# Windowed attention with a gated feed-forward: where the first unit's queries are issued, and on which engine a weight's first decoding step may run

## The chip, the cores and the metric

The kernel runs on one core of one Trainium2 chip. The metric is device time in microseconds (us). The median of three runs of the kernel before is 1043.59 us (1042.27 to 1043.75).

## The reference

```python
scores = scale * q @ k.T                       # 8 batches, 8 heads, 576 tokens, 64 wide
mask = (rel >= 0) & (rel < 128)                # rel = query position - key position
scores = where(mask, scores - slopes[h] * abs(rel), -1e9)
attn = exp(scores - max(scores)); attn = attn / (sum(attn) + 1e-9)
x = (attn @ v), heads side by side             # 4608 tokens x 512
out = (sigmoid(x @ w_gate) * (x @ w_val)) @ w_out   # 512 -> 1536 -> 512
```

The queries, keys and values are float32. The three weights are float64 and reach the chip as pairs of 32-bit words.

## The kernel before

The program works on 32 attention units; a unit is one batch and one pair of heads, laid out as nine blocks of 128 columns (1152 columns). For each unit it loads keys (`kr`, 576 KB), queries (`qr`, 320 KB) and values (`vr`, 288 KB). PE computes the scores of four blocks at a time in the early units (L387), DVE merges the two halves of the window (L400) and reduces (L408), ACT takes the exponential (L411), ACT or DVE scales (L431, L432), PE transposes three blocks (L436), ACT or DVE copies them out (L181, L182), POOL spreads them over a triangle layout (L447), and PE multiplies with the values (L473). The unit's result goes to DRAM (`xs`).

The feed-forward runs in three passes over the hidden units. The first takes 2 of 12 slices of the weights while the attention is still running (L523 for gate and value, L561 for the output projection): its matmuls fill PE's gaps. The two others take 5 slices each and all tokens, with a Strassen-like product (L667) and the output projection (L561).

A slice of a weight is a float64 tile of 128x512 that has to be decoded into float32 first. `decode` (L291) loads the raw words into one of two buffers (`wraw`), scales the high words on ACT (L300), shifts them left on DVE (L301), and or-s bits from the low and the high words in on DVE (L304, twice). Then the value is split into two parts: a cast (L181 on ACT or L182 on DVE) and a subtraction (L190). The tile `wbits`, of which there are two, is free again after the subtraction. 36 slices are decoded: 6 for the first pass, 15 for each later one.

The order of all instructions is written by a planner, `Graph` (L61 to L150), before the program is built. Each operation has a due time (`want`), a cost, and one or more ways, that is engines with a cost each. `order` (L97) is greedy: among all operations whose inputs are planned, it takes the one with the smallest key. The key holds the start time on the engine, the cost above the cheapest way, and a small penalty (0.1 for DVE) for a way that is not the first:

```python
key = (s + cost - least + (YIELD[e] if k else 0.0), o.want, o.seq)
...
gap = (o.start - free["PE"] - 0.2) // (0.25 if free["PE"] > 5.0 else 0.45)
...
moved = max(moved, o.start + 1.7) + o.size
```

Where PE would sit idle early in the plan, the planner puts filler matmuls of the identity there (`warm`, L246), so many as fit its own gap. A DMA's landing is planned from one running total of bytes (`moved`, L127) at 220 KB per us of plan (350 for weights). All DMAs are issued by `move` (L185) on SP's queue, in the order of the plan. The planner knows nothing of the set-up that DVE does at the start (L215 to L232), nor of ACT's table load.

`load` (L354) issues a unit's loads. For the first unit, keys and queries come in two parts each, cut at block 3; the values follow. The scores of blocks 0 to 3 read the keys of blocks 0 to 3, so they need both parts of the keys and the first part of the queries; blocks 4 to 7 need the second part of the queries too.

Of the kernel before, what the change touches and what calls it, by code (L numbers as in the profile page):

```python
# [19 lines left out]
NBLK = TOK // P  # L20
DM, DFF = 512, 1536
# [30 lines left out]
def as32(ap):  # L52
    return ap.bitcast(F32)
# [97 lines left out]
def dve_cost(n, psum=False, two=False):  # L151
    return 0.07 + n * (0.00104 if psum or two else 0.00053)


def act_cost(n, psum=False):
    return (0.05 if psum else 0.1) + n * 0.00084
# [3 lines left out]
def attention_gated_ffn(ctx: ExitStack, tc: tile.TileContext, qd, kd, vd, wg, wv, wo, out):  # L160
    nc = tc.nc
    ctx.enter_context(tc.manual_schedule())
    g = Graph()
# [10 lines left out]
    def T(pool, name, shape, dtype, tag=None):  # L174
        if name not in made:
            made[name] = pool.tile(shape, dtype, tag=tag or name, name=name)
        return made[name]
# [4 lines left out]
              ways=[("DVE", dve_cost(n, psum), not psum, lambda: nc.vector.tensor_copy(out(), src()))])  # L182


    def move(out, src, reads, writes, want, kb, fast=False, release=0.0):  # L185
        g.add("SP", 0.6, lambda: nc.sync.dma_start(out(), src()), reads, writes, want, size=kb / (350.0 if fast else 220.0), release=release)

    def minus(out, a, b, n, reads, writes, want, psum=False, pool=True):
        way = ("POOL", 0.1 + n * 0.00223, True, lambda: nc.gpsimd.tensor_tensor(out(), a(), b(), op=ALU.subtract))
# [101 lines left out]
    def decode(src, fc, bits, kb, keys, want, release=0.0):  # L291
        s = raws[0] % NRAW
        raws[0] += 1
        kr = ("wraw", s)
        if src.dtype == F32:
            move(lambda: as32(bits()), lambda: src[fc], keys, [kb], want, 256, False, release)
            return
        raw = lambda: T(moe, f"wraw{s}", [P, DM, 2], I32)
        move(lambda: raw().rearrange("p f t -> p (f t)"), lambda: src[fc].bitcast(I32), [], [kr], want, 512, True, release)
        g.add("ACT", act_cost(DM), lambda: nc.scalar.mul(as32(bits()), as32(raw()[:, :, 1]), 2.0 ** -112), [kr, *keys], [kb], want)  # L300
        g.add("DVE", dve_cost(DM), lambda: nc.vector.tensor_scalar(  # L301
            bits(), bits(), 3, None, op0=ALU.logical_shift_left), [], [kb], want, port=True)
        for word, scalar, o0 in ((0, 29, ALU.logical_shift_right), (1, -0x80000000, ALU.bitwise_and)):
            g.add("DVE", dve_cost(DM, two=True), lambda word=word, scalar=scalar, o0=o0: nc.vector.scalar_tensor_tensor(  # L304
                bits(), raw()[:, :, word], scalar, bits(), op0=o0, op1=ALU.bitwise_or), [kr], [kb], want, port=True)
# [7 lines left out]
    def prepare(w, src, kind, i, want):  # L313
        sb = bitn[0] % 2
        bitn[0] += 1
        bits = lambda: T(moe, f"wbits{sb}", [P, DM], I32)
        kb = ("wbits", sb)
        decode(src, w.fcs[i], bits, kb, w.keys(FC2), want)
        parts(lambda: w.tile(kind, 0)[:, i], lambda: w.tile(kind, 1)[:, i], lambda: as32(bits()), DM, [kb, *w.keys(FC2)],
              (w.name, kind, 0, i), (w.name, kind, 1, i), want)  # L320
# [32 lines left out]

    def load(u):  # L354
        want = u.when(-NBLK)
        cuts = (0, 3, NBLK) if u.n == 0 else (0, NBLK)
        for h, (b0, b1) in enumerate(zip(cuts, cuts[1:])):
            sl, q0, q1 = slice(b0 * P, b1 * P), (b0 + 1) // 2, (b1 + 1) // 2
            move(lambda sl=sl: kraw(u)[:, sl], lambda sl=sl: kd[u.b, u.p, :, sl], [], [("kr", u.l, i) for i in range(b0, b1)],
                 want, 64 * (b1 - b0))  # L360
            move(lambda q0=q0, q1=q1: qraw(u)[:, q0:q1], lambda q0=q0, q1=q1: qd[u.b, u.p, :, q0:q1], [],
                 [("qr", u.l, i) for i in range(2 * q0, 2 * q1)], want, 64 * (q1 - q0))
        move(lambda: vraw(u), lambda: vd[u.b, u.p], [], [("vr", u.l)], want, 288)


# [233 lines left out]
    def prepare2(w, i, want, release=0.0):  # L599
        s = bitn[0] % 2  # L600
        bitn[0] += 1
        kg, kt = ("wbits", s), "tt"
        gt = lambda: T(moe, f"wbits{s}", [P, DM], I32)
        tt = lambda: T(moe, "tt", [P, 6, 2 * P], F32)
        decode(wg, w.fcs[i], gt, kg, w.keys(i), want, release)
        decode(wv, w.fcs[i], lambda: tt()[:, 0:2].rearrange("p a f -> p (a f)").bitcast(I32), kt, w.keys(i), want, release)
        g0, g1, v0, v1 = (lambda: as32(gt())[:, 0:2 * P], lambda: as32(gt())[:, 2 * P:], lambda: tt()[:, 0], lambda: tt()[:, 1])
        t = [lambda k=k: tt()[:, 2 + k] for k in range(4)]
        for o, a, b in ((t[0], v0, g0), (t[1], v1, t[0]), (t[2], v1, v0), (t[3], g1, t[1])):
            minus(o, a, b, 2 * P, [kg], [kt], want)  # L610
        for a, b, src, k in ((0, 2, lambda: as32(gt()).rearrange("p (a f) -> p a f", a=2), kg), (2, 7, lambda: tt()[:, 1:], kt)):
            parts(lambda a=a, b=b: w.tile2(i, 0)[:, a:b], lambda a=a, b=b: w.tile2(i, 1)[:, a:b], src, (b - a) * 2 * P,
                  [k, *w.keys(i)], ("w2", i, 0, a), ("w2", i, 1, a), want)
# [105 lines left out]
    for n in range(NSLOT - 1):  # L719
        load(units[n])  # L720
    at = 0
    for u in units:
        if u.n + NSLOT - 1 < len(units):
            load(units[u.n + NSLOT - 1])
        while at < (u.n + 1) * NBLK:
            n = RUN // 2 if at < SOON * NBLK else RUN
            scores(stream[at:at + n])
            at += n
        if u.n == 0:
            todo = [(src, kind, i) for i0 in range(0, FC1, GRP) for src, kind in ((wg, "g"), (wv, "v")) for i in range(i0, i0 + GRP)]  # L730
            for k, (src, kind, i) in enumerate(todo + [(wo, "o", i) for i in range(FC1)]):
                prepare(w1, src, kind, i, W0 + WSTEP * k)
        if u.p == NPAIR - 1:
            while todo1 and (todo1[0] + 1) * NB <= (u.b + 1) * S:
                if todo1[0] >= LATE and banks[0] == 2:
                    banks[0] = 8
                    g.add("PY", 0.0, lambda: None, [], [TP, TAIL], FIRST)
                ffn(todo1.pop(0), w1)
# [84 lines left out]
```

## Time and profile before

| | us |
|---|---|
| median of three runs | 1043.59 |
| the profiled execution | 1042.42 |
| its span, first to last instruction | 1040.7 |
| PE busy | 1026.2 |
| DVE busy | 732.0 |
| ACT busy | 530.6 |
| POOL busy | 115.8 |

The span is what lies between the first and the last instruction of the profiled execution; the execution's own time holds 1.7 us more. Busy time is the union of an engine's instructions. A busy PE is not a PE at its peak, since the ends of matmuls are modelled; filler matmuls count as busy too. The granted clock of TensorE was 1.0 of full speed (the 2.4 GHz level) in every stretch. A matmul of float32 in the attention leaves two records in the trace. In the rows below, "x16" after an operation is the number of records, and the bracket at the end of a row of the timeline is the idle time of the engine just before it and what ended it.

### The profile page before, as it was taken

To read this page: it belongs to the slowest core of one execution; us is meant where nothing else is said; L and a number is where in the kernel's file an instruction comes from. 1 tells how busy PE (TensorE), PEld (TensorE's weight loads), DVE (VectorE), ACT (ScalarE), POOL (GpSimd) and SP (SyncE) were. 2 spreads that over 40 slices of the span, in tenths; PEclk is the share of its full clock that TensorE was granted. 3 is DMA by queue.
4 is the path that set the end of the run, shared out by engine and by line. 5 is a ranking of instruction groups with operands and counts; after the bars stand their busy time and mean duration, and the time that the engine had idled before them with its cause. 6 is when DMAs were issued, how large, how long until landed. Compare 5 with 4: busy or idle time off the path is not lost.

```text
span 1040.7 us, 17441 instructions
## 1 busy us (share of the span) xinstructions
PE 1026.2 (99%) x6024; PEld 913.4 (88%) x6024; DVE 732.0 (70%) x2031; ACT 530.6 (51%) x1477; POOL 115.8 (11%) x208
## 2 busy tenths in 40 slices
PE   9899999999999999999999999999999999999998
PEld 7677788787878998989899999989898989999897
DVE  7998888798899884554746475999556474747352
ACT  6898688898945551524334243635243333415140
POOL 2333233443411000000000000010000000000000
PEclk9999999999999999999999999999999999999999
DMA  8757577856556615041412305261503122040303
GB/s 285 250 191 262 184 249 223 297 168 254 184 192 213 222 51 182 1 152 31 137 47 81 102 17 186 82 233 52 163 20 118 65 96 88 26 157 1 122 1 102
DMA packets 74729, 142.70 MB, mean 137 GB/s; under 512 B 7312, under 2 KB 30224, under 8 KB 74640
## 3 DMA queue, kind: packets, MB, share of 16 engines
q1 hardware_dynamic: 74640, 141.58, 40.8%
q8 instruction: 47, 0.77, 0.3%
q14 instruction: 42, 0.34, 0.1%
HBM read 103.81 MB, written 37.75 MB: 136 GB/s over the span
## 4 chain that ended last, share of the span: by engine, by line
PE 88%; DVE 7%; ACT 3%; issue 1%; DMA 0%; POOL 0%; SPq 0%; ACTq 0%; DVEq 0%; POOLq 0%
PE mm L667 38%; PE mm L561 26%; PE mm L523 9%; PE mm L473 5%; PE mm L387 5%; PE mm L436 3%; ACT pb L411 1%; DVE wbits L304 1%; DVE mm L674 1%; ACT both L181 0%; DVE w2s L190 0%; DMA kr<-in_k_dram 0%; DVE hidden L190 0%; DVE tt L190 0%; DVE tt L304 0%
## 5 line engine op out<-in xcount | busy, mean ns | idle before, releaser
L667 PE MATMUL mm<-later,w2s 128*128 128x384 f32 x1800 | 332.0, 334 | 0.0
L667 PEld LDWEIGHTS mm<-later,w2s 128*128 128x128 f32 x1800 | 314.7, 188 | 1.1
L561 PE MATMUL mm<-w2o,hidden 128*128 128x512 f32 x1080 | 249.2, 390 | 0.0
L561 PEld LDWEIGHTS mm<-w2o,hidden 128*128 128x128 f32 x1080 | 202.4, 188 | 40.8
L678 ACT ACTIVATE sg<-mm 128x384 f32<-128x384 f32 x120 | 59.0, 493 | 145.6 <-PE mm L667 98.6
L181 ACT COPY a<-mm 128x384 f32<-128x384 f32 x60 | 28.8, 480 | 195.2 <-PE mm L667 194.5
L447 POOL TENSOR_SCALAR_AFFINE_SELECT pt<-both 128x384 f32<-128x384 f32 x192 | 105.0, 571 | 180.3 <-ACT both L181 164.0
L523 PE MATMUL mm<-first 128*128 128x512 f32 x432 | 111.6, 401 | 0.0
L566 DVE SCALAR_TENSOR_TENSOR ob<-mm,pi 128x512 f32<-128x512 f32 x72 | 49.5, 689 | 72.8 <-PE mm L561 39.0
L523 PEld LDWEIGHTS mm<-first 128*128 128x128 f32 x432 | 77.8, 188 | 15.5 <-issue 1.0
L674 DVE TENSOR_TENSOR mm<-mm,a 128x384 f32<-128x384 f32 x60 | 33.8, 564 | 75.6 <-PE mm L667 75.6
L411 ACT ACTIVATE pb<-pb,st 128x128 f32<-128x128 f32 x216 | 84.7, 398 | 2.5 <-DVE st L408 2.3
L667 PE MATMUL mm<-xc,w2s 128*128 128x384 f32 x360 | 73.0, 337 | 0.2 <-DVE p L674 0.2
L667 PE MATMUL mm<-later_o,w2s 128*128 128x384 f32 x360 | 72.3, 335 | 0.0
L473 PEld LDWEIGHTS mm<-pt,vr 128*64 128x64 f32 x832 | 61.2, 137 | 12.7 <-issue 8.7
L473 PE MATMUL mm<-pt,vr 128*64 128x256 f32 (+2 forms) x832 | 67.4, 306 | 0.6 <-POOL pt L447 0.6
L667 PEld LDWEIGHTS mm<-xc,w2s 128*128 128x128 f32 x360 | 63.4, 188 | 1.8 <-DVE p L674 0.8
L667 PEld LDWEIGHTS mm<-later_o,w2s 128*128 128x128 f32 x360 | 63.2, 188 | 0.5 <-ACT u L181 0.5
L181 ACT COPY both<-mm 128x384 f32<-128x384 f32 x95 | 45.2, 475 | 27.4 <-PE mm L436 16.6
L561 PE MATMUL mm<-first_o,early_h 128*128 128x512 f32 x216 | 57.1, 402 | 1.2 <-ACT early_h L181 0.7
L387 PE MATMUL mm<-kr,qr 64*128 64x256 f32 (+1 forms) x396 | 55.4, 382 | 0.2 <-DMA kr<-in_k_dram 0.2
L400 DVE COPY_PREDICATED mm<-early_h,mm 128x256 f32<-128x256 int32 (+1 forms) x144 | 49.0, 391 | 8.8 <-PE mm L387 8.3
(117 smaller groups left out, 1347.9 us busy)
## 6 DMA issues: line engine op xcount, KB each, us to landing
part<-ob SPq DMA_DIRECT2D x72, 256.0 KB, 4.3
pi<-part SPq DMA_DIRECT2D x72, 256.0 KB, 3.3
later_xr<-xs SPq DMA_DIRECT2D x16, 768.0 KB, 4.7
kr<-in_k_dram SPq DMA_DIRECT2D x21, 576.0 KB, 5.0
vr<-in_v_dram SPq DMA_DIRECT2D x32, 288.0 KB, 3.3
xs<-xt SPq DMA_DIRECT2D x32, 288.0 KB, 3.0
out_dram<-ob SPq DMA_DIRECT2D x36, 256.0 KB, 2.1
qr<-in_q_dram SPq DMA_DIRECT2D x21, 320.0 KB, 5.3
```

What stands on the lines that cost most here:

```text
L181: g.add("ACT", act_cost(n, psum), lambda: nc.scalar.copy(out(), src()), reads, writes, want, release=release, ways=[("DVE", dve_cost(n, ps ...
L387: nc.tensor.matmul(sp[bank_of(r, a)][:, a % 2, lo:], qraw(u)[rows, i // 2], kraw(u)[rows, (i - 1) * P + lo:(i + 1) * P], start=True, stop= ...
L400: g.add("DVE", dve_cost((a1 - a0) * P, psum=True), lambda b=b, a0=a0, a1=a1: nc.vector.copy_predicated(sp[b][:, a0:a1, P:], before[:, a0:a ...
L411: g.add("ACT", 0.39, lambda: nc.scalar.activation(pb()[:, e], pb()[:, e], AF.Exp, bias=st()[:, e:e + 1], scale=-1.0, accum_out=st()[:, 3 + ...
L447: nc.gpsimd.affine_select(pt(u)[:, f0:f0 + 2 * n - 1:2, :], both(), [[0, n], step], cmp, 0.0, base=0, channel_multiplier=mult)
L473: nc.tensor.matmul(to()[e * D:(e + 1) * D, a - e * S - t0:b - e * S - t0], vraw(u)[:, c], seen, start=first, stop=last, skip_group_check=True)
L523: nc.tensor.matmul(mm[s], w.tile(kind, wi)[:, i, c * P:(c + 1) * P], x()[:, c, :], start=(k == 0 and c == 0), stop=(k == 2 and c == KC - 1))
L561: nc.tensor.matmul(mm[s], hcol(x, i, w is w1)[:, ts], w.tile("o", wi)[:, i, :], start=(i == 0 and k == 0), stop=(i == n - 1 and k == 2))
L566: g.add("DVE", dve_cost(DM, psum=True), lambda: nc.vector.scalar_tensor_tensor(ob(), mm[s], 0.5, pi(), op0=ALU.mult, op1=ALU.add), [("mm", ...
L667: nc.tensor.matmul(mm[b][:, 0:N2], w.tile2(i, wp)[:, wk, c * P:(c + 1) * P], combo(k, xp)[:, c], start=(start and c == 0 and j == 0), stop ...
L674: g.add("DVE", dve_cost(N2, psum=True), lambda: nc.vector.tensor_tensor(o(), bk(b)(), a(), op=ALU.add), [("mm", b), *reads] if okeys else ...
L678: g.add("ACT", act_cost(N2, psum=True), lambda: nc.scalar.activation(sg[h](), bk(b)(), AF.Tanh, scale=0.5), [("mm", b)], [("sg", h)], F)
```

## The change

The first unit's keys and queries are loaded in three parts each, cut at blocks 2 and 4. Its query loads are issued from ACT's queue, all other loads stay on SP. And the first step of decoding gets a second way: beside ACT, the planner may put it on DVE.

```diff
-    def move(out, src, reads, writes, want, kb, fast=False, release=0.0):
-        g.add("SP", 0.6, lambda: nc.sync.dma_start(out(), src()), reads, writes, want, size=kb / (350.0 if fast else 220.0), release=release)
+    def move(out, src, reads, writes, want, kb, fast=False, release=0.0, queue="SP"):
+        start = nc.sync if queue == "SP" else nc.scalar
+        g.add(queue, 0.6, lambda: start.dma_start(out(), src()), reads, writes, want, size=kb / (350.0 if fast else 220.0), release=release)
...
-        g.add("ACT", act_cost(DM), lambda: nc.scalar.mul(as32(bits()), as32(raw()[:, :, 1]), 2.0 ** -112), [kr, *keys], [kb], want)
+        scaled = lambda: (as32(bits()), as32(raw()[:, :, 1]), 2.0 ** -112)
+        g.add("ACT", act_cost(DM), lambda: nc.scalar.mul(*scaled()), [kr, *keys], [kb], want,
+              ways=[("DVE", dve_cost(DM), True, lambda: nc.vector.tensor_scalar_mul(*scaled()))])
...
-        cuts = (0, 3, NBLK) if u.n == 0 else (0, NBLK)
+        cuts = (0, 2, 4, NBLK) if u.n == 0 else (0, NBLK)
+        queue = "ACT" if u.n == 0 else "SP"
...
-                 [("qr", u.l, i) for i in range(2 * q0, 2 * q1)], want, 64 * (q1 - q0))
+                 [("qr", u.l, i) for i in range(2 * q0, 2 * q1)], want, 64 * (q1 - q0), queue=queue)
```

In the planner's costs the step takes 0.53 on ACT (`act_cost(512)`) and 0.34 on DVE (`dve_cost(512)`). The parts of the keys are now 128, 128 and 320 KB, those of the queries 64, 64 and 192 KB; before they were 192 and 384, and 128 and 192 KB.

## Rows read from the trace of the kernel before

**Rows 1.** Busy time of each engine in stretches of the whole program: the stretch and its length, then busy us and number of instructions for PE, PEld, DVE, ACT and POOL, the granted clock, the share of the DMA engines and GB/s.
```profile
0.00:20.00 20.00, 18.41 (x127) 15.04 (x129) 15.22 (x88) 10.45 (x42) 4.70 (x15) 1.00 0.84 303
20.00:60.00 40.00, 35.69 (x297) 26.68 (x293) 37.62 (x188) 37.00 (x149) 14.29 (x25) 1.00 0.73 246
60.00:150.00 90.00, 87.15 (x668) 69.20 (x668) 78.11 (x404) 75.63 (x296) 31.62 (x61) 1.00 0.65 217
150.00:250.00 100.00, 100.00 (x780) 80.53 (x779) 83.66 (x430) 85.62 (x320) 39.81 (x74) 1.00 0.75 252
...
300.00:640.00 340.00, 339.96 (x1746) 312.63 (x1745) 221.14 (x359) 132.45 (x258) 4.47 (x4) 1.00 0.35 116
640.00:710.00 70.00, 69.85 (x375) 65.92 (x374) 68.08 (x121) 38.76 (x72) 3.95 (x3) 1.00 0.45 149
```

**Rows 2.** The chain of work that ended last, in order of time, one of its longest pieces: start, length, what.
```profile
408.94 35.49 PE mm L667 x204
```

**Rows 3.** The same chain in its first 13 us.
```profile
1.71 4.73 DMA kr<-in_k_dram
...
6.48 1.66 PE mm L387 x10
8.14 2.88 PE mm L246 x24
...
11.79 1.11 PE mm L387 x7
```

**Rows 4.** SP's instructions at the start, in order of time: the issue of the first unit's loads. Start, length of the issue, what.
```profile
0.80 0.38 SPq L186 DMA_DIRECT2D kr<-in_k_dram  x1
...
1.71 0.42 SPq L186 DMA_DIRECT2D kr<-in_k_dram  x1
2.17 0.43 SPq L186 DMA_DIRECT2D qr<-in_q_dram  x1
2.65 0.43 SPq L186 DMA_DIRECT2D vr<-in_v_dram  x1
```

**Rows 5.** PE before the first scores, from the timeline; and the second part of the queries in the list of DMA issues (size, us from issue to landing).
```profile
1.43 3.78 PE L246 MATMUL mm<-ident 128*128 128x128 f32 x16 [1.43 <-POOL ident masks.py:199]
...
qr<-in_q_dram SPq DMA_DIRECT2D x1, 192.0 KB, 4.8
```

**Rows 6.** ACT and DVE at the start, from the timeline: ACT's table load, the end of DVE's set-up, DVE's first work on scores, ACT's first exponential.
```profile
0.80 1.28 ACT L411 ACT_TABLE_LOAD   x1 [0.80 <-PEq L807]
...
4.33 1.30 DVE L232 TENSOR_SCALAR early_h<-early_h 128x640 f32<-128x640 f32 x3
...
6.36 0.30 DVE L400 COPY_PREDICATED mm<-early_h,mm 128x128 f32<-128x128 int32 x1 [0.73 <-PE mm L387]
...
7.88 0.40 ACT L411 ACTIVATE early_h<-early_h,st 128x128 f32<-128x128 f32 x1 [5.80 <-DVE st L408]
```

**Rows 7.** The timeline from 13 to 19 us: ACT's two longest waits there, and PE's filler between them.
```profile
13.37 0.48 ACT L181 COPY both<-mm 128x384 f32<-128x384 f32 x1 [1.50 <-PE mm L436]
...
14.32 2.27 PE L246 MATMUL mm<-ident 128*128 128x128 f32 x18
...
18.65 0.48 ACT L181 COPY both<-mm 128x384 f32<-128x384 f32 x1 [1.05 <-PE mm L436]
```

**Rows 8.** The chain of work that ended last between 20 and 25 us: the first step of decoding on it.
```profile
21.16 0.57 ACT wbits L300
...
24.23 0.57 ACT wbits L300
```

**Rows 9.** DVE between 24 and 39 us, from its timeline: its two idle times, the last decoding step of the first weight and that weight's cast; and ACT's first steps of decoding at 39.83 and 44.05.
```profile
24.26 0.28 DVE L426 TENSOR_SCALAR st<-st 128x3 f32<-128x3 f32 x1 [0.60 <-ACT pb L411]
...
31.31 0.68 DVE L304 SCALAR_TENSOR_TENSOR wbits<-wraw,wbits 128x512 int32<-128x512 int32 x1
...
36.58 0.27 DVE L426 TENSOR_SCALAR st<-st 128x3 f32<-128x3 f32 x1 [0.47 <-ACT pb L411]
...
38.29 0.42 DVE L182 CAST first<-wbits 128x512 fp32r<-128x512 f32 x1
...
39.83 0.69 ACT L300 ACTIVATE wbits<-wraw 128x512 f32<-128x512 f32 x1
...
44.05 0.65 ACT L300 ACTIVATE wbits<-wraw 128x512 f32<-128x512 f32 x1
```

**Rows 10.** The first two decoding steps by their lines, over the whole program: count, then shortest, median and longest in ns, first and last start in us.
```profile
L300 ACT ACTIVATE wbits<-wraw x26: 648/672/706, 21.1 to 712.9; 128x512 f32<-128x512 f32 x26
...
L301 DVE TENSOR_SCALAR wbits<-wbits x26: 398/419/741, 21.8 to 713.8; 128x512 int32<-128x512 int32 x26
```

**Rows 11.** The chain of work that ended last from 643 to 704 us: its first piece on DVE, one of L301 and one of L304; and PE's row of the timeline where the chain goes back to PE.
```profile
643.58 0.57 DVE mm L674
...
659.35 0.34 DVE wbits L301
...
660.15 0.60 DVE wbits L304
...
703.79 1.31 PE L667 MATMUL mm<-xc,w2s 128*128 128x384 f32 x6 [0.15 <-DVE p L674]
```

**Rows 12.** The first step of decoding in the stretch from 640 to 720 us.
```profile
L300 ACT ACTIVATE wbits<-wraw x8: 661/680/703, 642.9 to 712.9; 128x512 f32<-128x512 f32 x8
L300 ACT ACTIVATE tt<-wraw x4: 667/676/681, 649.3 to 688.9; 128x512 f32<-128x512 f32 x4
```

## The prediction

> **What bounds the kernel now.** I read the busy time by stretch first [rows 1]. From 150 to 250 us PE is busy all the time, from 300 to 640 for 339.96 of 340 us, from 640 to 710 for 69.85 of 70. Its pace there is a full one: the chain of waits has 204 matmuls of one kind in 35.49 us [rows 2], 174 ns each with nothing between. PE's work is fixed by the reference, so a change can shorten the program only where PE has holes or plays filler. That is the beginning: PE is idle 1.59 us before 20 us, 4.31 us from 20 to 60, 2.85 us from 60 to 150. Before 20 us much of "busy" is warm-up matmuls (L246), which compute nothing. In 20 to 60 us ACT has 37.00 and DVE 37.62 of 40 us: these two, not PE, are the bound of the head, and from about 150 us on everything is shifted by whatever the head takes.
>
> Second, the chain of waits at the start [rows 3]. It goes through the landing of the second part of the keys (to 6.44 us), the ten matmuls that need it, 24 filler matmuls for 2.88 us, and then the next scores at 11.79. The first part of the keys is not on it. Third, the issue times on SP [rows 4], and what PE, DVE and ACT do until then [rows 5 to 7]. Fourth, the chain from 20 to 45 us and where the weights' first step (L300) stands in it [rows 8, 9]. Last, the stretch from 643 to 704 us, where the second set of weights is decoded [rows 11].
>
> **The change, part by part. Loads of the first unit.** Five DMAs on SP (keys, queries, keys, queries, values) become four on SP (keys of 2, 2 and 5 blocks, values) and three on ACT (queries). Costs: three issues of about 0.43 us [rows 4] on ACT. ACT loads its table until 2.08 us and then waits 5.80 us for DVE [rows 6], so 1.3 us of issuing is hidden; without that cover it would cost 1.3 us. SP's later issues come one slot, 0.47 us, sooner (the values at 2.17 and not 2.65 us).
>
> What the first four blocks need shrinks from 704 KB (all but the last queries) to 384 KB. DVE, however, is in its set-up until 5.63 us (4.33 + 1.30) and now starts on the scores at 6.36 [rows 6]. So it gains at most 0.73 us there; with less waiting behind it, the first exponential on ACT comes some 1.2 us before 7.88. This is not on the chain. The chain needs blocks 4 to 7, that is the last keys and queries, and these complete the same 896 KB as before. After them PE plays filler up to the time at which the planner expects the second unit's queries; its transfer model gets the same bytes in the same order up to there, so the expected time stays. The gain on the path is what the second landing gains. The queries landed at about 6.97 (issued at 2.17, 4.8 us to landing) [rows 4, 5]. Their issue moves from 2.17 to about 1.7 us if ACT issues ahead of its table load (0.80 plus two slots of 0.46): up to 0.5 us sooner. If the table load goes first, the third issue is at 2.08 + 2 x 0.46, about 3.0 us, 0.8 us later than now. In front of the filler a further gap or two is rounded down, worth about one filler matmul of 0.24 us (two records of 0.12, 2.88 us by 24) [rows 3]. I take -0.3 us, ends -0.5 and +0.8: nearer to the gain, because the last keys keep their issue time of 1.71 with 64 KB less in them.
>
> A rule speaks against this part. The Trainium skill, "DMA: Bandwidth & Descriptors", section "Issuing engines are not separate DMA queues", says that transfers issued by different engines share the same 16 DMA engines and that a second issuer saves only issue time. Issue time alone would be the -0.5 us end, bytes alone would be 0; no row here shows two issuers.
>
> **The first step of decoding.** A weight of 128x512 takes one step on ACT (L300, median 672 ns, 0.57 us of its chain at a time), one on DVE (L301, 419 ns) and two more (L304) [rows 8, 10]. The first step may now run on DVE. No row shows that; the nearest are L301 (one source, contiguous) and L304 (two sources, every other word): 0.34 us in DVE's full queue, as L301's piece of the chain, to 0.60, as L304's [rows 11]. I take 0.34, as the step has one source.
>
> The Trainium skill, "VectorE: DVE Perf Modes", section "What auto-detection actually checks", lets one-source instructions from and to SBUF run at two elements a cycle on conditions that name the outermost dimension and not the step. By that the strided step costs what L301 does; no row here shows a strided one-source step.
>
> The planner takes DVE when DVE is free no later than 0.09 us after ACT (0.53 - 0.34 on ACT against a penalty of 0.1). Where DVE's queue is full, ACT keeps the step. The ACT way also gets a handicap of 0.19 in the key that it did not have, so the step is passed over while ACT has ready work. Behind it wait L301, L304, the cast and the subtraction, and then the buffer. In the head this is covered: the cast of the first weight runs at 38.29, 6.3 us after its last decode step (31.31 + 0.68) [rows 9].
>
> Of six such steps in the head, two lie on the chain while ACT carries it, 0.57 us each at 21.16 and 24.23 [rows 8]. DVE was idle 0.60 us before 24.26 and 0.47 before 36.58 [rows 9], room for two steps of 0.34 (0.68 in 1.07). Two more (39.83, 44.05) run while DVE carries the chain; if moved, they cost 0.34 each. So the ends are -1.14 and +0.68. I take one of the two moved with profit: -0.6 us.
>
> After 150 us: 0. PE has no holes, and what ACT saves there, nobody waits for.
>
> **The order itself.** The planner is greedy; another way in one step reorders hundreds after it. This can give back or lose part of PE's holes from 20 to 150 us (4.31 + 2.85 = 7.2 us) [rows 1]. No row tells which sign; I count a quarter, 1.8 us, as an error on both sides.
>
> **The sum.** -0.3 - 0.6 = -0.9 us. The profiled execution took 1042.42 us (span 1040.7 and 1.7 around it): it would be 1041.5. The median of the three runs stands 1.17 us above that execution, so I put the forecast at 1043.59 - 0.9 = 1042.7 us. Alone it has 1040.6 to 1044.8 (1.8 us of order, and some of the other ends).
>
> **Rivals.** (a) *The change does nothing to the path*: the second landing stays at about 7 us, because bytes and not issue times set it, and the planner leaves the steps of the head on ACT, as DVE's queue is as full as ACT's (37.62 against 37.00 of 40 us) [rows 1]. Time 1043.6. For it: filler fixed by the planner [rows 3]. Against it: DVE does have the two gaps [rows 9].
>
> (b) *The head packs better than I count*: both early steps leave ACT (-1.14), the landing gains its 0.5, and transposes of the first blocks, done sooner, take away one of ACT's early waits (1.50 us at 13.37, 1.05 at 18.65) [rows 7], say 1.05. Together -2.7: 1040.9 us. Against it: at 14.32 PE plays filler again for the planner's expected transfers [rows 7], which keeps the early pace.
>
> (c) *Slower: DVE becomes the bound at 643 to 704 us.* There DVE has 68.08 of 70 us [rows 1], the chain runs along DVE from 643.58 until PE, at 703.79, has waited 0.15 us for DVE [rows 11]: DVE has no slack left against PE. Each step that the planner gives to DVE here costs 0.34 us of the end. It decides from about six such steps (2.1 us); with all twelve of the stretch [rows 12] it is 4.1 us: 1047.7. Against it: with a full DVE queue the key prefers ACT, which has 38.76 of 70 us.
>
> **How the numbers follow.** Forecast 0.45 (of it 0.04 below and 0.02 above the bounds), (a) 0.17, (b) 0.25 (0.01 within), (c) 0.13 (0.02 within). A measurement of this kernel can tell about 0.2%, 2.1 us, from no change: below 1041.5 is faster, above 1045.7 slower. That gives faster 0.28, same 0.59, slower 0.13. The predicted time is that of the forecast, 1042.7 us. The range reaches down over (b), with its order error partly, to 1039.6 and up to 1045.6, which leaves out most of (c) and the deepest part of (b), 2 in 10.
>
> **What would show it.** In the profile after: queries issued on ACT, at about 0.8 us or behind the table load; ten filler records in place of 16 ahead of the first scores [rows 5] (the planner's gap there falls from 3.8 to 2.3 us of its own time, five matmuls of 0.45 where there were eight); the first exponential near 6.7 us; the scores of the second unit still at 11 to 12 us. L301's line and the first step on DVE at about 0.42 us each; in the head one to three of six on DVE; from 643 to 704 few or none. PE idle from 20 to 60 us down by about a microsecond. It is wrong if the scores of the second unit come over 1 us sooner, if PE waits for DVE near 700 us, or if PE's holes up to 150 us change by over 2 us through order alone.

## The result: 6.4 us slower

| | before | after |
|---|---|---|
| median of 6 runs, us | 1042.22 (1041.8 to 1043.75) | 1048.57 (1046.8 to 1050.44) |
| profiled execution, us | 1042.42 | 1047.89 |
| its span, us | 1040.7 | 1046.2 |

The ratio is 1.0063, 95% interval 1.0053 to 1.0074: slower by over 0.2%, and outside the range of the prediction.

**Where the time is lost.** Busy time of each engine by stretch, the changed kernel, columns as in [rows 1]; one more stretch is shown, 360 to 380 us, in which PE was busy for all 20.00 us before.
```profile
0.00:20.00 20.00, 17.57 (x122) 14.42 (x122) 14.47 (x87) 10.97 (x42) 3.96 (x14) 1.00 0.81 289
20.00:60.00 40.00, 35.75 (x285) 26.81 (x283) 35.54 (x194) 36.79 (x155) 14.96 (x27) 0.96 0.72 248
60.00:150.00 90.00, 86.63 (x682) 69.14 (x679) 77.33 (x392) 72.31 (x271) 34.67 (x64) 1.00 0.66 215
150.00:250.00 100.00, 98.41 (x769) 78.26 (x768) 83.47 (x423) 83.85 (x318) 40.27 (x69) 1.00 0.72 240
250.00:300.00 50.00, 49.51 (x341) 40.22 (x340) 42.27 (x159) 35.78 (x121) 19.07 (x30) 1.00 0.49 171
...
360.00:380.00 20.00, 18.80 (x105) 17.58 (x104) 18.05 (x30) 9.98 (x21) 0.00 (x0) 1.00 0.47 151
...
640.00:710.00 70.00, 70.00 (x373) 65.87 (x372) 62.90 (x109) 36.40 (x66) 6.24 (x4) 1.00 0.45 147
```
The kernel before from 250 to 300 us, a stretch that [rows 1] don't show:
```profile
250.00:300.00 50.00, 48.18 (x340) 38.57 (x335) 43.61 (x142) 37.91 (x117) 16.92 (x28) 1.00 0.43 143
```
PE's holes grow by 0.84 us before 20 us and by 0.52 from 60 to 150; from 20 to 60 they stay, but the clock is below 1. From 150 to 250 there are 1.59 us of holes where there were none, and from 250 to 300 they shrink from 1.82 to 0.49. At 360 to 380 us there are 1.20 us of holes where there were none. From 640 to 710, the stretch of the prediction's rival (c), PE is busier than before.

Holes in a timeline can understate a wait, since the ends of matmuls are modelled. Two landmarks measure it in another way: when PE is done with the first pass, and how long the next 60 matmuls, all of the second pass, take from start to start. First the kernel before, PE's timeline at the change of passes.
```profile
349.09 1.23 PE L667 MATMUL mm<-later,w2s 128*128 128x384 f32 x6
350.15 2.92 PE L561 MATMUL mm<-first_o,early_h 128*128 128x512 f32 x12
352.91 10.59 PE L667 MATMUL mm<-later,w2s 128*128 128x384 f32 x60
363.34 1.20 PE L667 MATMUL mm<-later_o,w2s 128*128 128x384 f32 x6
```
The changed kernel, the same view (L667 is L671, L561 is L565).
```profile
349.51 5.64 PE L565 MATMUL mm<-first_o,early_h 128*128 128x512 f32 x24
354.98 8.74 PE L671 MATMUL mm<-later,w2s 128*128 128x384 f32 x48
363.97 0.62 PE L671 MATMUL mm<-later,w2s 128*128 128x384 f32 x2 [0.25 <-ACT later L181]
365.50 2.32 PE L671 MATMUL mm<-later,w2s 128*128 128x384 f32 x10 [0.92 <-DVE later L191]
367.67 1.20 PE L671 MATMUL mm<-later_o,w2s 128*128 128x384 f32 x6
```
Before, the first pass ends at 350.15 + 2.92 = 353.07 us; less the 1.06 us in which six matmuls of the second pass had been done ahead, 352.0. After, it ends at 349.51 + 5.64 = 355.15: **3.1 us late**. Then the next 60 matmuls take 363.34 - 352.91 = 10.43 us before and 367.67 - 354.98 = 12.69 after: **2.3 us more**. Together that is the whole loss of this execution: the chain's last run of output projections starts at 1016.54 before and 1021.90 after, 5.4 us later.
```profile
1021.90 20.45 PE mm L565 x90
```

**Why PE waits at 364 us.** DVE's timeline of the kernel before, its only idle time over 1.5 us there.
```profile
340.89 0.56 DVE L182 CAST xc<-later_xr 128x768 fp32r<-128x768 f32 x1 [1.88 <-DMA later_xr<-xs]
341.49 0.96 DVE L190 TENSOR_TENSOR xc<-later_xr,xc 128x768 fp32r<-128x768 f32 x1
```
The changed kernel.
```profile
345.25 0.43 DVE L303 TENSOR_SCALAR wbits<-wraw 128x512 f32<-128x512 f32 x1 [4.76 <-DMA wraw<-in_moe_w_out_dram]
...
355.00 0.95 DVE L191 TENSOR_TENSOR xc<-later_xr,xc 128x768 fp32r<-128x768 f32 x1
...
364.50 0.95 DVE L191 TENSOR_TENSOR later<-xsum,later 128x768 fp32r<-128x768 f32 x1
```
After, a decoding step stands in front in DVE's queue whose weight is still in flight; DVE idles 4.76 us, and the preparation of the tokens (`xc`) behind it comes at 355.00 and not at 341.49. But for 0.92 us ahead of 347.06 DVE's timeline shows no wait from there until 368 (20.80 us busy from 347.06 to 368), and PE waits for the subtraction of 364.50.

**The head.** The chain of waits at the start, to hold against [rows 3]; ACT's timeline, to hold against [rows 6]; PE's fillers ahead of the first scores [rows 5].
```profile
1.72 5.23 DMA qr<-in_q_dram
...
7.00 1.18 PE mm L391 x8
...
12.37 1.71 PE mm L391 x13
```
```profile
0.80 1.38 ACTq L187 DMA_DIRECT2D qr<-in_q_dram  x3
2.21 1.28 ACT L415 ACT_TABLE_LOAD   x1 [2.21 <-issue]
6.56 0.40 ACT L415 ACTIVATE early_h<-early_h,st 128x128 f32<-128x128 f32 x1 [3.07 <-DVE st L412]
```
```profile
1.43 2.50 PE L247 MATMUL mm<-ident 128*128 128x128 f32 x10 [1.43 <-POOL ident masks.py:199]
```
ACT issues the three query loads ahead of its table load; the first exponential is 1.32 us sooner. But the third part of the queries, issued 0.45 us sooner than the second part was, lands at 6.95, as the second part did before, and the second unit's scores come 0.6 us later than in [rows 3].

The first decoding step by its lines, on ACT and on DVE; beside [rows 10].
```profile
L302 ACT ACTIVATE wbits<-wraw x17: 666/674/696, 21.3 to 718.8; 128x512 f32<-128x512 f32 x17
```
```profile
L303 DVE TENSOR_SCALAR wbits<-wraw x9: 395/420/605, 26.5 to 345.3; 128x512 f32<-128x512 f32 x9
...
L303 DVE TENSOR_SCALAR tt<-wraw x2: 415/416/418, 248.8 to 301.3; 128x512 f32<-128x512 f32 x2
```
Of 36 steps 11 moved, five of them among the first six. Two of those on DVE's timeline, which answer to the steps at 39.83 and 44.05 in [rows 9]:
```profile
46.88 0.42 DVE L303 TENSOR_SCALAR wbits<-wraw 128x512 f32<-128x512 f32 x1
...
52.13 0.42 DVE L303 TENSOR_SCALAR wbits<-wraw 128x512 f32<-128x512 f32 x1
```
They start 7.1 and 8.1 us later than they did on ACT.

### The profile page after: what moved, and what is told of

Its sections match the earlier page's. It is cut to its first block, busy times and chain, and to the rows that moved or that the text cites. A ratio compares the mean times of both kernels' runs of the same rounds, so it can differ in the third digit from the quotient of the medians.

```text
span 1046.2 us, 17430 instructions
## 1 busy us (share of the span) xinstructions
PE 1027.8 (98%) x6024; PEld 913.8 (87%) x6024; DVE 730.1 (70%) x2041; ACT 525.4 (50%) x1464; POOL 123.6 (12%) x211
## 4 chain that ended last, share of the span: by engine, by line
PE 89%; DVE 5%; ACT 4%; DMA 1%; issue 1%; ACTq 0%; DVEq 0%; SPq 0%
PE mm L671 40%; PE mm L565 28%; PE mm L527 8%; PE mm L391 5%; PE mm L477 5%; PE mm L440 3%; ACT pb L415 1%; ACT both L181 1%; DVE wbits L307 1%; DMA qr<-in_q_dram 1%; DVE first L191 0%; ACT pb L435 0%; DVE mm L404 0%; DVE pb L436 0%; DMA wraw<-in_moe_w_out_dram 0%
## 5 line engine op out<-in xcount | busy, mean ns | idle before, releaser
L671 PE MATMUL mm<-later,w2s 128*128 128x384 f32 x1800 | 332.5, 335 | 1.2 <-DVE later L191 0.9
L671 PEld LDWEIGHTS mm<-later,w2s 128*128 128x128 f32 x1800 | 314.5, 188 | 3.4 <-DVE later L191 1.5
L565 PE MATMUL mm<-w2o,hidden 128*128 128x512 f32 x1080 | 249.2, 390 | 0.0
L565 PEld LDWEIGHTS mm<-w2o,hidden 128*128 128x128 f32 x1080 | 202.4, 188 | 40.8
L671 PE MATMUL mm<-xc,w2s 128*128 128x384 f32 x360 | 73.1, 338 | 0.0
L671 PE MATMUL mm<-later_o,w2s 128*128 128x384 f32 x360 | 72.1, 334 | 0.5 <-ACT u L181 0.5
L671 PEld LDWEIGHTS mm<-xc,w2s 128*128 128x128 f32 x360 | 63.5, 188 | 1.5 <-DVE p L678 0.3
L671 PEld LDWEIGHTS mm<-later_o,w2s 128*128 128x128 f32 x360 | 63.2, 188 | 0.8 <-ACT u L181 0.8
L565 PE MATMUL mm<-first_o,early_h 128*128 128x512 f32 x216 | 57.1, 403 | 1.8 <-ACT early_h L181 1.3
L391 PE MATMUL mm<-kr,qr 64*128 64x256 f32 (+1 forms) x396 | 56.5, 391 | 0.7 <-DMA qr<-in_q_dram 0.5
```

Source lines behind the costliest of these rows:

```text
L391: nc.tensor.matmul(sp[bank_of(r, a)][:, a % 2, lo:], qraw(u)[rows, i // 2], kraw(u)[rows, (i - 1) * P + lo:(i + 1) * P], start=True, stop= ...
L565: nc.tensor.matmul(mm[s], hcol(x, i, w is w1)[:, ts], w.tile("o", wi)[:, i, :], start=(i == 0 and k == 0), stop=(i == n - 1 and k == 2))
L671: nc.tensor.matmul(mm[b][:, 0:N2], w.tile2(i, wp)[:, wk, c * P:(c + 1) * P], combo(k, xp)[:, c], start=(start and c == 0 and j == 0), stop ...
```

## The experiments

Four explanations stand against each other. *DVE's work*: eleven steps of 0.42 us on an engine that is full in the head. *The queue*: issuing from ACT. *The handicap*: the planner's key puts the ACT way 0.19 back, so decoding is late. *The order*: any change of a cost or a due time makes the greedy planner write another order, and this one is worse, whatever the moved work costs. Ratios are against runs of the kernel before on the same chip.

**One half of the change at a time.** e1 has the loads as in the change and the step on ACT only; e2 has the second way, and the loads as before.
```diff
e1 -              ways=[("DVE", dve_cost(DM), True, lambda: nc.vector.tensor_scalar_mul(*scaled()))])
e2 -        cuts = (0, 2, 4, NBLK) if u.n == 0 else (0, NBLK)
e2 -        queue = "ACT" if u.n == 0 else "SP"
e2 +        cuts = (0, 3, NBLK) if u.n == 0 else (0, NBLK)
e2 +        queue = "SP"
```


> Only the loads are changed (three parts, queries on ACT's queue); the first decoding step stays on ACT as before. Theory T (the loss comes from the second way: the planner puts the second to sixth step of the first pass 2 to 7 us later, so the matmuls of the feed-forward that fill PE's holes from 50 to 95 us come later): 1041 to 1044 us, no loss from 50 to 95. Rival L (the loads: the second landing is at 7.00 instead of 6.48 and the second unit's scores at 12.30 instead of 11.72, and all follows): about 1048, most of the loss of 6 us. Rival O (any other order loses, because the one before is an unusually good one): 1044 to 1048, with holes in other places.

> Only the second way for the first decoding step; loads as before. T: 1047 to 1049, as the full change, with the steps late in the head (second at about 26 us, third at about 47, fourth at about 52) and PE's holes from 50 to 95. L: 1042. O: 1044 to 1049.

e1: 1049.62 us, 1.0070 (1.0057 to 1.0083). e2: 1046.39, 1.0045 (1.0032 to 1.0059). The losses are 7.8 and 4.6 us, and both together lose 6.4: they don't add up. Terms that are each priced and summed can't describe this. And e1 loses no less than the whole change, with no decoding step moved.

**The handicap alone; the new order without DVE's work.** e3 is the kernel before, with 0.19 added to the key of the first step and no second way. e4 is the changed kernel in its own order, but each first step that was planned on DVE is issued on ACT.
```diff
...
e3 +                    key = (s + cost - least + o.late + (YIELD[e] if k else 0.0), o.want, o.seq)
...
e4 -              ways=[("DVE", dve_cost(DM), True, lambda: nc.vector.tensor_scalar_mul(*scaled()))])
e4 +              ways=[("DVE", dve_cost(DM), True, lambda: nc.scalar.mul(*scaled()))])
```


> The kernel before with one thing: the planner's key for the first decoding step carries the handicap of 0.19 that the second way brings, but there is no second way, so all 36 steps stay on ACT and the loads are as before. T: the steps are passed over in the head as in the full change, and it loses most of what the full change loses up to 300 us: 1044 to 1047. A rival D (the loss is DVE's added work: eleven steps of 0.34 us on an engine that is full): 1042, nothing is added to DVE. L: 1042.

> The full change with its order of all instructions, but each first step that the planner gives to DVE is issued on ACT at the same place of the order. T and O: the order is what costs, so 1048 to 1050 (eleven steps of 0.57 us on ACT may add up to a microsecond). D: DVE is relieved of eleven steps, 1043 to 1045.

e3: 1046.52 us, 1.0046 (1.0033 to 1.0058): as much as the second way loses, with nothing on DVE. e4: 1051.32, 1.0087 (1.0074 to 1.0101): taking DVE's new work away makes the kernel no faster, so DVE's work isn't the cause of the 6.4 us. That e4 is slower than the change isn't shown: in three of its four executions the mean granted clock was 0.997, and the one at 1.0 took 1049.07 us, inside the range of the changed kernel.

**The old order with DVE's work, or with the queue.** e5 is the kernel before in its own order, with the eleven steps that the changed kernel runs on DVE issued there. e6 is the kernel before with the first unit's queries on ACT's queue, in two parts as before; PE's, DVE's and POOL's order doesn't change.
```diff
e5 +        g.add("ACT", act_cost(DM), lambda mul=nc.vector.tensor_scalar_mul if raws[0] - 1 in (1, 2, 3, 4, 5, 6, 9, 13, 14, 18, 20) else nc.scalar.mul: mul(as32(bits()), as32(raw()[:, :, 1]), 2.0 ** -112), [kr, *keys], [kb], want)
...
e6 +        queue = "ACT" if u.n == 0 else "SP"
...
```


> The order of the kernel before, word for word, with the first step of eleven weights (the eleven that the full change gives to DVE) issued on DVE at ACT's place in the order; loads as before. Theory O (an order other than the one before loses, and the added work is cheap): 1041 to 1043 us. D (DVE's added eleven steps of 0.34 us cost time): 1043 to 1046.

> The first unit's queries on ACT's queue, in two parts as before, no second way; the planner's order on PE and DVE stays that of the kernel before. O: 1041 to 1042.5 us, as two queue issues come some 0.5 us sooner and the landing is set by bytes. L (issuing queries on ACT makes the second landing late, 7.00 instead of 6.48): 1043 or more, with the second unit's scores 0.5 us later.

e5: 1043.84 us, 1.0015 (1.0006 to 1.0024), a loss of 1.7 us between the medians. Most of it goes with TensorE's clock: the four executions with a mean granted clock of 0.999 or more took 1042.11 to 1043.01 us, 0.5 us above before in the middle, and the seven at 0.997 or 0.998 took 1043.71 to 1045.54. e6: 1041.33, 0.9994 (0.9985 to 1.0002), no loss. PE's timeline at the start of e6:
```profile
5.14 2.73 PE L390 MATMUL mm<-kr,qr 64*128 64x128 f32 x16
7.80 2.95 PE L247 MATMUL mm<-ident 128*128 128x128 f32 x24
...
11.45 1.13 PE L390 MATMUL mm<-kr,qr 64*128 64x256 f32 x8
...
qr<-in_q_dram ACTq DMA_DIRECT2D x1, 192.0 KB, 4.1
```
The last row is from e6's list of DMA issues. The first scores show no wait for the second landing, which comes 1.6 us sooner than before: the second queries, issued in ACT's second slot at about 1.25 us, took 4.1 us, so they land at about 5.35 and not 6.97. The second unit's scores start at 11.45, against 11.72 on the timeline of before; 24 fillers stand between, as planned. That 0.3 us is not clear of the scatter: in the eight profiled kernels that load the first unit in two parts from SP (before, e2, e3, e5, e7, e8, e10, e11) they start at 11.16 to 11.90. The four with three parts and ACT's queue (after, e1, e4, e9) have them at 12.30 to 13.41, later than all of these, as the third part of the queries takes 5.2 to 6.4 us to land. So the queue by itself didn't lose, and the cut in three, issued as it was, makes the head start later; three parts with all loads on SP were not run, nor three parts in the old order.

**Another order with nothing else changed.** e7 gives the due times of the first pass's weights another start; e8 gives the planner another price for ACT. Neither touches an instruction, a queue or the list of ways.
```diff
e7 -W0, WSTEP = 20.0, 2.0
e7 +W0, WSTEP = 19.0, 2.0
e8 -    return (0.05 if psum else 0.1) + n * 0.00084
e8 +    return (0.05 if psum else 0.1) + n * 0.00085
```


> The kernel before with one number of the planner changed that nothing physical hangs on: the due time of the weights of the first pass is 19 instead of 20. All loads, engines and amounts of work stay; the planner's order changes. O: it loses as the others do, 1044 to 1050 us. Against O (the changed parts themselves cost): within a microsecond of 1042.

> The kernel before with the planner's price of one element on ACT at 0.00085 instead of 0.00084. All loads, engines with a choice and amounts of work stay; the planner's order changes. O: 1044 to 1050 us. Against O: within a microsecond of 1042.

e7: 1048.27 us, 1.0060 (1.0048 to 1.0073). A due time that is 1 us earlier costs as much as the whole change. e8: 1042.77, 1.0007 (0.9998 to 1.0016). e8 hides more than its time tells; PE's timeline:
```profile
346.76 2.92 PE L561 MATMUL mm<-first_o,early_h 128*128 128x512 f32 x12
349.52 6.78 PE L667 MATMUL mm<-later,w2s 128*128 128x384 f32 x38
...
363.34 2.04 PE L667 MATMUL mm<-later,w2s 128*128 128x384 f32 x10 [1.00 <-DVE later L190]
366.69 1.32 PE L667 MATMUL mm<-xc,w2s 128*128 128x384 f32 x6 [1.31 <-DVE p L674]
```
The first pass ends at 349.68 less 1.06 = 348.6, 3.4 us sooner than before. All of it is lost again at the start of the second pass, where PE waits for DVE: behind the next 84 matmuls PE stands at 367.85 us, before at 367.50.

**Two orders joined.** So far "the order" only names what is left over. If it is the cause, the two losses belong to two stretches of the order and can be moved one by one. e9 keeps the changed kernel's order up to 304 us of the plan (parts, queue and steps on DVE included) and takes the order and engines of the kernel before from there. e10 is the mirror, with all first steps on ACT. e11 joins e8's order, up to 300 us, with that of before. `TAIL` is the second order as a list.
```diff
-        steps = [(o.start, 0, o.seq, o.emit) for o in self.order()]
...
+        tail = _np.frombuffer(zlib.decompress(base64.b85decode(TAIL)), "<u2").tolist()
+        ops = [o for o in self.order() if o.start < 304.0]
...
+        steps = [(o.start, 0, o.seq, o.emit) for o in ops]
+        steps += [(304.0 + i, 0, code >> 2, self.ops[code >> 2].ways[code & 3][4]) for i, code in enumerate(tail)]
```


> The changed kernel in its own order up to 304 us of the plan (parts, ACT's queue and the first steps on DVE included); from there on the instructions stand in the order, and on the engines, of the kernel before. Theory 'the order loses at two places' (some 2.5 us before 300 us, some 2.5 at the start of the second feed-forward pass, where PE waits for DVE at 364 to 366 us): the second loss goes, about 1045.0. Rival 'all is lost before 300 us and the wait at 364 only shows that DVE is late': PE still waits there, about 1048.

> The mirror: the kernel before in its own order up to 304 us of the plan, from there on in the order of the changed kernel (the first decoding step stays on ACT throughout). Theory 'two places': only the loss at the start of the second pass appears, about 1044.7. Rival 'all is lost before 300 us': no loss, 1042.2.

> The kernel before planned with ACT's price 0.00085 up to 300 us of the plan (an order that had lost some 3.5 us less of PE's time by 300 us than that of the kernel before, and gave all of it back from 355 to 375), from there on the order of the kernel before. Theory 'the order loses and wins at separate places': the gain stays, about 1038.8. Rival 'DVE's preparation of the second pass sets the end of that stretch, and a PE that comes sooner only waits longer': 1042 to 1042.8.

PE's timeline of e9, where L571 and L677 are the two lines:
```profile
353.38 2.92 PE L571 MATMUL mm<-first_o,early_h 128*128 128x512 f32 x12
356.14 10.59 PE L677 MATMUL mm<-later,w2s 128*128 128x384 f32 x60
366.57 1.20 PE L677 MATMUL mm<-later_o,w2s 128*128 128x384 f32 x6
```
e10, PE and then DVE:
```profile
346.50 5.85 PE L567 MATMUL mm<-first_o,early_h 128*128 128x512 f32 x24
352.19 6.78 PE L673 MATMUL mm<-later,w2s 128*128 128x384 f32 x38
...
362.98 2.32 PE L673 MATMUL mm<-later,w2s 128*128 128x384 f32 x10 [0.93 <-DVE later L196]
365.13 1.20 PE L673 MATMUL mm<-later_o,w2s 128*128 128x384 f32 x6
```
```profile
344.02 0.43 DVE L307 TENSOR_SCALAR wbits<-wbits 128x512 int32<-128x512 int32 x1 [5.75 <-ACT wbits L306]
```
e11:
```profile
348.33 2.92 PE L567 MATMUL mm<-first_o,early_h 128*128 128x512 f32 x12
351.09 10.59 PE L673 MATMUL mm<-later,w2s 128*128 128x384 f32 x60
361.51 1.20 PE L673 MATMUL mm<-later_o,w2s 128*128 128x384 f32 x6
```

| | first pass ends, against before | next 60 matmuls, of the second | median, us | ratio (95%) |
|---|---|---|---|---|
| before | 352.0 | 10.43 | 1041.87 | |
| after | +3.1 | 12.69 | 1048.57 | 1.0063 (1.0053 to 1.0074) |
| e9 | +3.2 | 10.43 | 1044.99 | 1.0028 (1.0016 to 1.0039) |
| e10 | +0.3 | 12.94 | 1044.43 | 1.0023 (1.0014 to 1.0032) |
| e11 | -1.8 | 10.42 | 1040.03 | 0.9983 (0.9974 to 0.9991) |

(Each ratio is against the runs of the kernel before on the same chip.) Each loss goes with its stretch: e9 loses 3.1 us, e10 2.6, together 5.7 of the changed kernel's 6.4. For the second stretch the order is shown as the cause, since e10 changes nothing else. In the first, e9 also has the loads and the steps on DVE. In e10 DVE idles at the same place as after (5.75 us, now behind a step on ACT), though nothing before 304 us of the plan differs from the kernel before. e11 gained less than expected: 1.8 us and not 3.4 are there at the end of the first pass, so by the traces the rest of e8's gain lay behind 300 us of the plan: PE has no hole from 250 to 300 us in e8 and 1.17 us in e11.

**The queue on the better order.** e12 is e11 with e6's edit.

> The kernel of the run before this one (planned with ACT's price 0.00085 up to 300 us, then the old order) with the first unit's queries, in two parts, issued on ACT's queue; the plan is the same instruction by instruction. Theory 'what is gained at the second landing stays, since no order changes': some 0.7 us off 1040.0, about 1039.3, the fastest of all. Rival 'a sooner landing is taken up by the next wait of the head': 1040.0.

1039.5 us, 0.9976 (0.9966 to 0.9986): faster than the kernel before by 0.24%, and the lowest median of all. PE's timeline of e12; the second unit's scores start at 11.24 in e11.
```profile
10.84 1.13 PE L396 MATMUL mm<-kr,qr 64*128 64x256 f32 x8
```
The 0.4 us are still there at the end of the first pass (349.76 against 350.19 by the landmark above). Between e11 and e12 the times differ by 0.5 us, with overlapping ranges of runs (1039.45 to 1041.26, 1039.11 to 1040.47) on two chips, so what the queue adds is not shown.

## Why the prediction was wrong

**The step that failed** is "The order itself". It said that another order could give back or lose part of PE's holes from 20 to 150 us and counted a quarter of them, 1.8 us, on both sides. Two things were wrong in it. The place: 2.3 us are lost at the start of the second pass, where [rows 1] show no hole at all and the prediction wrote "After 150 us: 0. PE has no holes". A stretch without holes can get some, as those at 150 to 250 and at 360 to 380 us did. The sentence was also wrong of the kernel before, which has 1.82 us of holes from 250 to 300 us, the stretch that [rows 1] leave out. The size: e7 moves 6.2 us (1048.27 against 1042.1) with no physical edit. Of the six kernels here in an order that the planner wrote anew (after, e1, e2, e3, e7, e8) five lose 4.6 to 7.8 us and one 0.7; none won, and e11 shows that there was 1.8 us to win. "No row tells which sign" treated it as even. None of the prediction's three signs of being wrong came, since they looked at other places: PE doesn't wait near 700 us, its holes up to 150 us grow by 1.3 us and not 2, and the second unit's scores come later and not sooner.

**"In the head this is covered"** isn't borne out. The 6.3 us behind the first weight's decoding [rows 9] were read as cover for all; the steps on the third and fourth weight came 7 to 8 us late, and e3, with the handicap alone, loses 4.7 us. How much of that is lateness and how much the new order behind it, these runs don't separate.

**The price of the step** came out in its busy time: 420 ns, as L301's 419; what one costs on the chain (the prediction's 0.34 us) no run shows by itself. The Trainium skill, "VectorE: DVE Perf Modes", section "What auto-detection actually checks", puts its conditions on the outermost dimension and not on the step; the trace agrees, 420 ns strided beside 419 contiguous [rows 10]. The gain worked out from the price (-0.6) didn't come: in the old order the same eleven steps on DVE lose 1.7 us (e5), or 0.5 in the executions at full clock. The count was wrong as well, five of the first six on DVE and not one to three.

**The loads** (-0.3, ends -0.5 and +0.8). As made, in three parts, the second unit's scores start 0.6 us late in the changed kernel and 0.9 to 1.7 us late in e1, e4 and e9 (12.30, 12.70, 12.62 and 13.41 against 11.72): the sign was wrong, and the last three lie beyond the +0.8 end. What the prediction missed is that the third part of the queries would take longer to land, 5.2 to 6.4 us and not 4.8. ACT issued ahead of its table load, ten fillers, the first exponential at 6.56 (6.7 was said): right. "The second unit still at 11 to 12 us" missed by 0.3. The section "Issuing engines are not separate DMA queues" of the Trainium skill's "DMA: Bandwidth & Descriptors" would leave the landing only the sooner issue, 0.45 us. With three parts that gain didn't come. With two the traces fit it: issued 0.92 us sooner from ACT, the 192 KB took 4.1 us in e6 and 4.2 in e12, at the lower end of the 4.2 to 4.8 us that they took when issued from SP.

**Rival (c)**, DVE as the bound from 643 to 704, was the wrong slow case: no first step went to DVE after 345.3 us, so its reason, that DVE has no slack there, wasn't put to the test. The place where DVE's order decided was the change of passes.

**Still open** is what loses the first 3.1 us. PE's holes from 0 to 360 us grow by 2.2 us, most of it (1.6) from 150 to 250. e9 shows that the loss belongs to the order, the loads or the steps before 304 us of the plan. e3 and e7 show that an order alone can lose as much, but no run has the changed kernel's head order without its loads, and no single wait was taken out.

## What to carry to other kernels

When a greedy planner writes the order of all engines, a change of one cost, way or due time is first a change of order. Run a neutral change of the planner's constants beside it: what it moves (here 0.7 and 6.2 us in two runs) is the size below which a local sum of terms says little. And an order can be cut and joined: the two stretches here lost and won on their own, and joining a good head to a good tail (e11) gave a faster kernel than any single edit that was run.

## What was not expected of the hardware

In the profiled execution of the changed kernel the clock of TensorE fell. Windows of 2 us; the columns are those of [rows 1].
```profile
50.00:52.00 2.00, 1.35 (x12) 1.00 (x11) 0.97 (x5) 1.87 (x9) 1.00 (x2) 1.00 0.47 101
52.00:54.00 2.00, 0.81 (x6) 0.50 (x3) 2.00 (x8) 2.00 (x9) 0.54 (x1) 0.86 0.66 83
54.00:56.00 2.00, 2.00 (x10) 1.19 (x8) 1.71 (x11) 2.00 (x9) 1.58 (x4) 0.50 0.89 340
56.00:58.00 2.00, 2.00 (x10) 1.31 (x10) 1.61 (x11) 1.29 (x7) 0.61 (x2) 0.79 1.02 416
```
After two windows in which PE was busy for 1.35 and 0.81 of 2 us, the granted clock is at 0.50, the 1.2 GHz level, and eight records of scores (L391) take 2.08 us where they took 1.13 at the full level at 51 us.

What this cost can be read against e9, which has the same order up to there and a clock of 1.00 from 20 to 60 us. In e9 the third part of the queries landed later still:
```profile
8.11 1.14 PE L397 MATMUL mm<-kr,qr 64*128 64x256 f32 x8 [1.33 <-DMA qr<-in_q_dram]
```
So e9 starts 1.1 us behind the changed kernel and is 1.1 us behind it at 48 us (49.03 against 47.93, the same product with the values). At 57 us it is 0.45 us ahead (56.40 against 56.85), at 150 us 0.18. The changed kernel lost some 1.5 us against e9 between 48 and 57 us; how much of that stays to the end these two executions don't tell, as e9 had lost its 1.1 us at the landing. A lower clock goes with a longer time in several kernels (e5 above), but it isn't the cause of the result: of 70 executions of the kernel before, run beside the experiments, one had a mean granted clock below 0.999, of six of the changed kernel three (1047.89, 1049.25 and 1050.44 us). Its other three took 1046.80, 1047.88 and 1050.30, still 5.7 us above before in the middle, and e3 and e10 lose at 0.999 or more in every execution.
